# Thresholded attention, then a gated mixture of attentions: first-stage scores as three rounded products, exponential without a bias operand, fewer buffers, another order

## Chip, cores and metric

One core of a Trainium2 chip runs the whole kernel. The metric is the device time of one execution in microseconds, as the median of several runs. Engines: TensorE (PE in the profile, PEld its weight loads), VectorE (DVE), ScalarE (ACT), GpSimd (POOL) and SyncE (SP, which issues most DMAs).

## What is computed

`q`, `k`, `v` are 8 batches x 8 heads x 576 queries x 64. The first stage is an attention that keeps only scores within `tau` of the row's maximum. Its output, heads side by side, is the input `x` (576 x 512 per batch) of a second stage: a gate chooses 2 of 4 "experts" for each row, and every expert is a causal attention of its own with 64 columns.

```python
def _attn_ref(q, k, v, tau):
    scale = 1.0 / np.sqrt(q.shape[-1])
    scores = scale * np.matmul(q, k.transpose(0, 1, 3, 2))
    thresh = np.max(scores, axis=-1, keepdims=True) - tau
    scores = np.where(scores >= thresh, scores, -1000000000.0)
    scores = scores - np.max(scores, axis=-1, keepdims=True)
    attn = np.exp(scores)
    attn = attn / (np.sum(attn, axis=-1, keepdims=True) + 1e-09)
    return np.matmul(attn, v).astype(np.float32)
...
    for e in range(E):                     # second stage, E = 4
        q = x @ wq[e]
        k = x @ wk[e]
        v = x @ wv[e]
        scores = scale * (q @ k.transpose(0, 2, 1))
        scores = np.where(causal, -1000000000.0, scores)
        ...
        ye = a @ v @ wo[e]
        out += mask * w * ye               # w: softmax of the two chosen gate logits
```

## The kernel before

**Tiling.** Two heads of a batch are a pair, 32 pairs in all (`pair(n)`). Of a pair's 576 queries, 512 make four strips of 128 (`s` = 0 to 3). The last 64 queries of two successive pairs share a fifth strip (`s == R`), which is done with the odd pair, so there are 128 whole strips and 16 such shared ones, called tails below. A strip has two score rows of 576 keys, one for each head.

**One strip.** `prep` loads keys and queries, transposes them on PE (64 x 64 pieces against `ident`) and copies them out of PSUM with ACT into `kx` and `qx`; the copy of `qx` multiplies by `qsc`. `scores` multiplies them in plain float32: for each half of the keys (288 columns) and each head one matmul, with the two heads on the two halves of the array's rows. A float32 matmul stands in the trace as two instructions, so a strip shows 8. Then DVE copies the scores out of PSUM and takes their minimum (`copied_min`, tile `sc`; scores are negated), POOL adds `tau` (`thr`), ACT applies a kinked line (`kinked`, Prelu, which throws everything under the threshold far down) and the exponential with its row sum (`exp`, with the column `tau_n` = -tau as bias), DVE inverts the sum and POOL scales the row. `transp` transposes the probabilities on PE, DVE copies them out (tile `pt`), and `attnv` multiplies by `v`. Its result is split by ACT and DVE into a rounded high part and the low rest (tiles `x`), float32r both.

**The tail** multiplies 64 columns of weights by 288: four 64 x 64 corners of the array work at once, two heads by two pairs.

**Second stage.** `moe(b)` follows each four pairs. All its products are three float32r matmuls, high x high, high x low, low x high (`HHL`), added up in PSUM.

**Order.** Nothing runs in the order of the text. `Plan` records every operation with its tiles, `arrange` places them with a list scheduler, and the tables `PLACE` and `PLACE_OP` shift the due times of units ("os10" is strip 1 of odd pairs, "ACT kx" ACT's writes to `kx`). `SLOTS` says how many buffers a tile name has. Engines then execute their own queues in that order; a waiting instruction holds up all behind it. `fill` puts idle matmuls (`still`) into the first 80 us where the plan leaves PE empty.

The time falls into a start of some 82 us, in which only the first stage has work, and then batches of some 103 us, in which pairs of the next batch run between the products of the second stage.

Of the kernel before, what the change touches and what calls it, by code (L numbers as in the profile page):

```python
# [1213 lines left out]
```

## Time and profile before

| what | value |
|---|---|
| time, median of 3 runs | 859.16 us (858.79 to 859.38) |
| span of the profiled execution | 856.8 us |
| busy: PE, PEld, DVE, ACT, POOL | 827.5, 705.9, 621.1, 712.3, 350.6 us |
| mean granted TensorE clock | 0.994 of full speed |

The profiled execution has no time of its own beside its span; the median lies 2.4 us over that span. Busy time of PE counts the modelled tail of each matmul, so short gaps between matmuls do not show as idle: the start of the next instruction is the better measure of what one costs.

### The profile page before, as it was taken

To read this page: it belongs to the slowest core of one execution; us is meant where nothing else is said; L and a number is where in the kernel's file an instruction comes from. 1 tells how busy PE (TensorE), PEld (TensorE's weight loads), DVE (VectorE), ACT (ScalarE), POOL (GpSimd) and SP (SyncE) were. 2 spreads that over 40 slices of the span, in tenths; PEclk is the share of its full clock that TensorE was granted. 3 is DMA by queue.
4 is the path that set the end of the run, shared out by engine and by line. 5 is a ranking of instruction groups with operands and counts; after the bars stand their busy time and mean duration, and the time that the engine had idled before them with its cause. 6 is when DMAs were issued, how large, how long until landed. Compare 5 with 4: busy or idle time off the path is not lost.

```text
span 856.8 us, 28908 instructions
## 1 busy us (share of the span) xinstructions
PE 827.5 (97%) x11478; PEld 705.9 (82%) x11478; DVE 621.1 (72%) x1990; ACT 712.3 (83%) x1880; POOL 350.6 (41%) x607
## 2 busy tenths in 40 slices
PE   7999999999999999999999999999999999999998
PEld 5677888779887888878887788878888788887897
DVE  2787677776868677786777768687677776877565
ACT  5998889988789868897799977998878987789565
POOL 3665345443435334353244523344334443344211
PEclk8999999999999999999999999999999999999999
DMA  4442201130210302112021211312112031100002
GB/s 96 121 98 57 52 19 46 28 81 21 68 45 25 91 14 82 45 32 72 13 71 44 58 45 30 81 31 72 31 55 58 16 78 36 38 16 16 15 26 75
DMA packets 108103, 42.77 MB, mean 50 GB/s; under 512 B 94784, under 2 KB 103232, under 8 KB 107968
## 3 DMA queue, kind: packets, MB, share of 16 engines
q1 hardware_dynamic: 106624, 40.63, 18.5%
q8 instruction: 90, 1.47, 0.7%
q10 hardware_dynamic: 1344, 0.30, 0.2%
q14 instruction: 45, 0.37, 0.1%
HBM read 31.47 MB, written 9.44 MB: 48 GB/s over the span
## 4 chain that ended last, share of the span: by engine, by line
PE 69%; ACT 18%; DVE 6%; POOL 3%; issue 3%; SPq 0%; DMA 0%; POOLq 0%; DVEq 0%; ACTq 0%
PE banks L587 58%; PE banks L1183 10%; ACT pp L699 7%; ACT pp L693 7%; DVE sc L682 2%; DVE pt L623 2%; POOL pp L649 2%; PE banks L1180 1%; POOL p L649 1%; ACT p L693 1%; ACT pt L621 1%; ACT x L621 1%; DVE col L648 1%; ACT ptt L621 1%; POOL col L649 1%
## 5 line engine op out<-in xcount | busy, mean ns | idle before, releaser
L649 POOL TENSOR_SCALAR pp<-pp,col 128x576 f32<-128x576 f32 x288 | 212.6, 748 | 201.5 <-DVE col L660 119.4
L699 ACT ACTIVATE pp<-sc,col 128x576 f32<-128x576 f32 x288 | 211.1, 776 | 24.5 <-POOL col L649 23.2
L682 DVE TENSOR_SCALAR_CACHE_REDUCE sc<-banks 128x576 f32<-128x576 f32 x288 | 208.0, 751 | 21.0 <-PE banks L587 18.8
L693 ACT ACTIVATE pp<-pp,tau_n 128x576 f32<-128x576 f32 x288 | 222.5, 778 | 0.2
L623 DVE COPY pt<-banks 128x512 f32<-128x512 f32 x288 | 182.8, 682 | 8.8 <-PE banks L1183 8.3
L587 PE MATMUL banks<-kx,qx 64*128 64x288 f32 (+1 forms) x1280 | 179.1, 424 | 7.0 <-DVE pt L623 4.6
L587 PE MATMUL banks<-pt,vm 128*64 128x128 f32 (+1 forms) x2560 | 156.3, 266 | 0.1
L587 PEld LDWEIGHTS banks<-pt,vm 128*64 128x64 f32 x2560 | 131.1, 137 | 16.2 <-DVE sc L682 4.9
L587 PEld LDWEIGHTS banks<-kx,qx 64*128 64x128 f32 (+1 forms) x1280 | 101.8, 177 | 45.0 <-DVE pt L623 11.0
L649 POOL TENSOR_SCALAR col<-col,tau_p 128x2 f32<-128x2 f32 x144 | 38.9, 270 | 232.1 <-DVE sc L682 154.1
L1183 PE MATMUL banks<-ident,pp 64*128 64x64 f32 x2624 | 121.6, 227 | 7.7 <-DVE sc L682 3.3
L1183 PEld LDWEIGHTS banks<-ident,pp 64*128 64x128 f32 x2624 | 105.2, 139 | 28.3 <-POOL pp L649 5.6
L693 ACT ACTIVATE p<-p,col 128x512 f32<-128x512 f32 (+2 forms) x138 | 82.1, 604 | 18.3 <-DVE col L677 18.2
L649 POOL TENSOR_SCALAR p<-p,col,gw 128x512 f32<-128x512 f32 (+3 forms) x117 | 71.2, 619 | 44.3 <-DVE gw L632 30.2
L648 DVE TENSOR_SCALAR col<-col 128x2 f32<-128x2 f32 (+1 forms) x224 | 46.7, 212 | 57.3 <-ACT pp L693 49.8
L677 DVE CUSTOM_DVE_ANT_0 p<-banks,mask 128x512 f32<-128x512 f32 (+2 forms) x138 | 68.2, 514 | 21.4 <-PE banks L587 17.1
L632 DVE TENSOR_TENSOR x<-banks,x 128x256 fp32r<-128x256 f32 (+1 forms) x96 | 31.1, 351 | 58.1 <-ACT x L621 57.9
L621 ACT ACTIVATE pt<-banks 128x384 f32<-128x384 f32 (+2 forms) x128 | 57.5, 512 | 7.6 <-PE banks L1183 6.3
L587 PE MATMUL banks<-wvh,x 128*128 128x260 f32 x320 | 61.1, 285 | 0.0
L587 PE MATMUL banks<-ptt,vtz 128*64 128x128 f32 (+1 forms) x640 | 58.9, 263 | 0.0
L693 ACT ACTIVATION_READ_ACCUMULATOR pp<-pp,tau_n 128x1 f32 x288 | 58.3, 202 | 0.0
L587 PE MATMUL banks<-x,wkh 128*128 128x288 f32 x256 | 54.7, 307 | 0.0
(111 smaller groups left out, 1358.4 us busy)
## 6 DMA issues: line engine op xcount, KB each, us to landing
ki<-in_k_dram SPq DMA_DIRECT2D x64, 128.0 KB, 2.8
vm<-in_v_dram SPq DMA_DIRECT2D x32, 256.0 KB, 3.0
qi<-in_q_dram SPq DMA_DIRECT2D x62, 128.0 KB, 2.8
out_dram<-st SPq DMA_DIRECT2D x29, 256.0 KB, 2.5
tk<-in_k_dram SPq DMA_DIRECT2D x64, 32.0 KB, 2.2
vtz<-in_v_dram SPq DMA_DIRECT2D x64, 16.0 KB, 2.1
out_dram<-st SPq DMA_DIRECT2D x8, 128.0 KB, 2.3
tq<-in_q_dram SPq DMA_DIRECT2D x31, 32.0 KB, 2.3
```

The costliest lines, as they stand in the source:

```text
L587: lambda o, x, y: nc.tensor.matmul(o, x, y, start=start, stop=stop))
L621: run(e, t, [dst], [src], lambda d, s: nc.scalar.activation(d, s, AF.Copy))
L623: run(e, t, [dst], [src], lambda d, s: nc.vector.tensor_copy(d, s))
L632: lambda d, a, b: (nc.vector if e == "DVE" else nc.gpsimd).tensor_tensor(d, a, b, op=op))
L648: return m.tensor_scalar(d, s, x_, None, op0=op0)
L649: return m.tensor_scalar(d, s, x_, y_, op0=op0, op1=op1)
L677: lambda o, a, i, m: nc.vector.tensor_tensor_reduce(o, i, m, 1.0, 3e38, ALU.add, ALU.min, a))
L682: lambda o, a, i: nc.vector.tensor_scalar(o, i, 1.0, None, op0=ALU.mult, op1=ALU.min, accum_out=a))
L693: return nc.scalar.activation(d, s, AF.Exp, scale=scale, **kw)
L699: lambda d, s, x: nc.scalar.activation(d, s, AF.Prelu, bias=x, scale=-1.0, alpha=1e36))
L1180: nc.tensor.matmul(banks[:, n, :256], still_[:, :P], still_[:, :1].to_broadcast([P, 256]), start=True, stop=True)
L1183: o.fn(*(r.place() for r in (*o.outs, *o.ins)))
```

## The change

- `kx` and `qx` become float32r with two planes, high and low. ACT writes the high plane as before (now rounded), and DVE subtracts it from PSUM for the low plane: `minus` for the keys, `stt` (times `qsc`, minus high) for the queries. These are five new DVE instructions a pair.
- `scores` makes three float32r matmuls (`HHL`) in place of one float32 matmul, so a strip is 12 instructions, the two heads still side by side.
- The tail's queries go to constant tiles `qz0` and `qz1` of 128 columns, of which one half holds a pair's 64 last queries and the other stays zero. The tail becomes 24 matmuls with 128 columns of weights, six sums of two pairs into each bank. ACT writes them with one more copy a pair (64 columns); the first copy of `qx` falls from 320 columns to 256.
- `exp` has no bias in the first stage any more (`tau_n` is gone; the factor cancels in the division), and `tau_p` is cut at 80 instead of 104.
- `pt` has 4 buffers instead of 6, `x` 11 instead of 12.
- All numbers of `PLACE` and `PLACE_OP` are new.

```diff
+TOP = 80.0
-         ... "pt": 6, ... "x": 12, ...
+         ... "pt": 4, ... "x": 11, ...
 PLACE = {
-    "LMo0": 5.6250437, "LMo1": 7.2007713, ...
+    "LMo0": 13.27813, "LMo1": 8.710187, ...
...
     def exp(dst, src, bias=None, accum=None, scale=1.0):
+        ref = isinstance(bias, Ref)
...
-            if bias is not None:
+            if ref:
                 kw["bias"] = r.pop(0)
...
-    scaled("DVE", tau_p, tau_t, 0.0, 104.0, op0=ALU.max, op1=ALU.min)
-    scaled("DVE", tau_n, tau_p, -1.0)
+    scaled("DVE", tau_p, tau_t, 0.0, TOP, op0=ALU.max, op1=ALU.min)
...
+    qz = [const(f"qz{i}", [P, 2, P], F32R) for i in range(2)]
+    for t in qz:
+        memset("POOL", t.bitcast(F32), 0.0)
...
-        kx, qx = plan.tile("kx", [P, SM + 3 * ST], F32), plan.tile("qx", [P, SM + P], F32)
+        kx, qx = plan.tile("kx", [P, 2, SM + 3 * ST], F32R), plan.tile("qx", [P, 2, SM], F32R)
...
+                outs.append(([qz[n % 2][:, i, heads[n % 2]] for i in range(2)], gs[0][:, R * D:(R + 1) * D]))
+            for (hi, lo), src in outs:
+                copy("ACT", hi, src, None if x is ki else qsc)
+                if x is ki:
+                    minus("DVE", lo, src, hi.bitcast(F32))
+                else:
+                    stt(lo, src, qsc, hi.bitcast(F32), ALU.mult, ALU.subtract)
...
+        mm = [(q_[:, x], kx[:, y]) for q_, kx in qks for x, y in HHL]
         for hf in range(2):
-            for j, rows in enumerate(heads):
-                o = hf * HS + (ST if j == 0 else 0)
-                for i, (qx, kx) in enumerate(qks):
-                    if s < R:
-                        matmul(sp[j][:, hf, :HS], qx[rows, s * P:(s + 1) * P], kx[rows, o:o + HS], True, True)
-                    else:
-                        matmul(sp[j][heads[i], hf, :HS], qx[rows, SM:SM + ST], kx[rows, o:o + HS], True, True)
+            for i, (x, y) in enumerate(mm):
+                for j, rows in enumerate(heads):
+                    o = hf * HS + (ST if j == 0 else 0)
+                    matmul(sp[j][:, hf, :HS], x[rows], y[rows, o:o + HS], i == 0, i == len(mm) - 1)
...
-            exp(e, e, bias=tau_n, accum=ss[:, j:j + 1])
+            exp(e, e, accum=ss[:, j:j + 1])
```

PE around a tail in the middle of the run, before (`pp`, `p` are probabilities of the first and second stage being transposed; the last two rows come three times more):

```order
L587 MATMUL banks<-kx_67,qx_65 128x288 x4
L1183 MATMUL banks<-ident,p_80 128x64 x10
L1183 MATMUL banks<-ident,pp_70 128x64 x16
L1183 MATMUL banks<-ident,pp_69 128x64 x2
L1183 MATMUL banks<-ident,pp_70 128x64 x2
L1183 MATMUL banks<-ident,pp_69 128x64 x16
L587 MATMUL banks<-kx_68,qx_66 128x288 x4
L587 MATMUL banks<-kx_67,qx_65 64x288
L587 MATMUL banks<-kx_68,qx_66 64x288
```

and the same place in the change (the last two rows come once more):

```order
L588 MATMUL banks<-kx_67,qx_65 128x288 x12
L1190 MATMUL banks<-ident,p_78 128x64 x16
L1190 MATMUL banks<-ident,pp_70 128x64 x16
L1190 MATMUL banks<-ident,pp_69 128x64 x2
L1190 MATMUL banks<-ident,pp_70 128x64 x2
L1190 MATMUL banks<-ident,pp_69 128x64 x16
L1190 MATMUL banks<-ident,p_79 128x64 x10
L588 MATMUL banks<-q_108,q_107 128x128 x6
L588 MATMUL banks<-kx_68,qx_66 128x288 x12
L588 MATMUL banks<-kx_67,qz_182 128x288 x6
L588 MATMUL banks<-kx_68,qz_183 128x288 x6
```

A strip is 12 rows instead of 4 (each of the 4 is two instructions in the trace), the tail 24 instead of 8; around them the sequence is the same, but for one product of the second stage (`q_108,q_107`) that now stands between.

ACT where the next even pair is prepared, before (`sc` are scores, `col` threshold and row sum):

```order
L621 ACTIVATE kx_67<-banks 128x5x64 x2
L693 ACTIVATE p_80,col_135<-p_80,col_134 128x128
L699 ACTIVATE pp_71<-sc_81,col_147 128x576
L699 ACTIVATE pp_71<-sc_83,col_147 128x576
L693 ACTIVATE pp_71,col_141<-pp_71,tau_n 128x576 x2
L621 ACTIVATE pt_121<-banks 128x6x64 x2
L619 ACTIVATE qx_65<-banks,qsc 128x5x64
L619 ACTIVATE qx_65<-banks,qsc 128x4x64
```

and in the change:

```order
L622 ACTIVATE kx_67<-banks 128x5x64 x2
L695 ACTIVATE pp_69,col_142<-pp_69 128x576
L701 ACTIVATE pp_71<-sc_81,col_144 128x576
L701 ACTIVATE pp_71<-sc_82,col_144 128x576
L695 ACTIVATE pp_71,col_145<-pp_71 128x576 x2
L620 ACTIVATE qx_65<-banks,qsc 128x4x64 x2
L622 ACTIVATE pt_116<-banks 128x6x64 x2
L622 ACTIVATE pt_117<-banks 128x6x64 x2
L622 ACTIVATE ptt_93<-banks 128x3x64 x2
L620 ACTIVATE qz_182<-banks,qsc 128x64
```

The exponentials have lost their second input, and the copy into `qz_182` has come in.

DVE at the same place, before (a run of score copies, row-sum inversions and copies of transposed probabilities, `st` is an output tile):

```order
L682 TENSOR_SCALAR sc_83,col_142<-banks 128x576
L660 RECIPROCAL col_124<-col_124 128x2
L623 COPY pt_86<-banks 128x8x64 x2
L648 TENSOR_SCALAR col_135<-col_135 128x2
L660 RECIPROCAL col_135<-col_135 128x2
L682 TENSOR_SCALAR sc_84,col_148<-banks 128x576
L623 COPY pt_89<-banks 128x8x64 x2
L682 TENSOR_SCALAR sc_82,col_148<-banks 128x576
```

and in the change:

```order
L683 TENSOR_SCALAR sc_82,col_140<-banks 128x576
L633 TENSOR_TENSOR kx_67<-banks,kx_67 128x5x64 x2
L624 COPY pt_86<-banks 128x8x64 x2
L649 TENSOR_SCALAR col_142<-col_142 128x2
L683 TENSOR_SCALAR sc_83,col_132<-banks 128x576
L661 RECIPROCAL col_142<-col_142 128x2
L683 TENSOR_SCALAR sc_84,col_132<-banks 128x576
L649 TENSOR_SCALAR col_145<-col_145 128x2
L624 COPY st_75<-banks 128x512
L672 SCALAR_TENSOR_TENSOR qx_65<-banks,qsc,qx_65 128x4x64 x2
```

The two low planes of `kx` and the two of `qx` now stand between the score copies and the `pt` copies for which PE waits; the fifth (`qz_182`) follows some rows later.

## Rows read from the trace of the kernel before

**Rows 1.** Head of the page: span, busy time of each engine.
```profile
span 856.8 us, 28908 instructions
...
PE 827.5 (97%) x11478; PEld 705.9 (82%) x11478; DVE 621.1 (72%) x1990; ACT 712.3 (83%) x1880; POOL 350.6 (41%) x607
```

**Rows 2.** Windows: stretch, length, busy PE, PEld, DVE, ACT, POOL (instructions), clock, DMA.
```profile
0.00:82.00 82.00, 72.24 (x936) 55.65 (x936) 52.53 (x150) 68.11 (x161) 44.08 (x89) 0.94 0.41 95
489.00:560.50 71.50, 71.50 (x954) 62.37 (x952) 50.97 (x166) 56.67 (x156) 24.50 (x41) 1.00 0.21 56
560.50:589.40 28.90, 26.70 (x429) 21.81 (x429) 23.19 (x76) 28.00 (x70) 16.20 (x29) 1.00 0.10 27
582.10:593.20 11.10, 10.20 (x169) 8.11 (x166) 8.80 (x25) 11.02 (x30) 8.21 (x14) 1.00 0.29 70
```

**Rows 3.** Chain that ended last: one same piece, two batches apart (start, length).
```profile
386.73 4.67 PE banks L587 x88
...
592.99 4.67 PE banks L587 x88
```

**Rows 4.** Timeline of PE: start, length with overlap, operation, count [idle before].
```profile
399.70 0.43 PE L587 MATMUL banks<-x,wqh 128*128 128x288 f32 x2
399.96 0.30 PE L587 MATMUL banks<-x,wql 128*128 128x288 f32 x1
...
565.87 0.80 PE L587 MATMUL banks<-q,q 64*128 64x384 f32 x6
566.51 1.13 PE L587 MATMUL banks<-kx,qx 64*128 64x288 f32 x8
567.48 0.47 PE L1183 MATMUL banks<-ident,p 64*128 64x64 f32 x10
...
571.86 1.20 PE L587 MATMUL banks<-kx,qx 64*64 64x288 f32 x16 [0.63 <-DVE pt L623]
573.00 1.09 PE L587 MATMUL banks<-pt,vm 128*64 128x128 f32 x16
```

**Rows 5.** Windows, PE's score matmuls (tile kx) alone: busy and count.
```profile
489.00:560.50 71.50, 13.24 (x96) 1.00 0.21 56
560.50:589.40 28.90, 8.53 (x64) 1.00 0.10 27
```

**Rows 6.** Weight loads by shape: busy us, mean ns | idle before.
```profile
L1183 PEld LDWEIGHTS banks<-ident,pp 64*128 64x128 f32 x2624 | 105.2, 139 | 28.3 <-POOL pp L649 5.6 <-DVE sc L682 5.6 <-issue 3.2
L587 PEld LDWEIGHTS banks<-kx,qx 64*128 64x128 f32 x1024 | 93.4, 188 | 32.5 <-issue 9.0 <-ACT kx L621 2.2 <-DVE pt L623 2.0
```

**Rows 7.** ACT by shape: busy us, mean ns | idle before.
```profile
L693 ACT ACTIVATE pp<-pp,tau_n 128x576 f32<-128x576 f32 x288 | 222.5, 778 | 0.2
...
L621 ACT ACTIVATE x<-banks 128x256 fp32r<-128x256 f32 x64 | 24.3, 380 | 3.2 <-PE banks L587 3.0
...
L619 ACT ACTIVATE qx<-banks,qsc 128x256 f32<-128x256 f32 x32 | 16.0, 499 | 0.0
...
L693 ACT ACTIVATE p<-p,col 128x128 f32<-128x128 f32 x30 | 12.3, 410 | 0.1
...
L621 ACT ACTIVATE x<-banks 128x64 fp32r<-128x64 f32 x32 | 5.4, 224 | 11.3 <-PE banks L587 11.3
...
L693 ACT ACTIVATE gw<-lg 128x20 f32<-128x20 f32 x8 | 1.7, 217 | 4.9 <-DVE col L648 4.9
```

**Rows 8.** ACT's first-stage exponentials from 0 to 82 us, then from 560.5 to 589.4.
```profile
L693 ACT ACTIVATE pp<-pp,tau_n x35: 758/767/803, 13.0 to 81.3; 128x576 f32<-128x576 f32 x35
...
L693 ACT ACTIVATE pp<-pp,tau_n x14: 758/784/823, 564.7 to 588.7; 128x576 f32<-128x576 f32 x14
```

**Rows 9.** DVE by shape: subtractions that read PSUM, for the low part of x.
```profile
L632 DVE TENSOR_TENSOR x<-banks,x 128x256 fp32r<-128x256 f32 x64 | 26.7, 418 | 37.9 <-ACT x L621 37.8
...
L632 DVE TENSOR_TENSOR x<-banks,x 128x64 fp32r<-128x64 f32 x32 | 5.7, 218 | 20.2 <-ACT x L621 20.1
```

**Rows 10.** Waits of DVE, longest first: total us, times, longest.
```profile
DVE x L632 <- ACT x L621: 57.9, 40, 2.4
```

More of the change, by code (lines that the diff above doesn't have):

```diff
@@ L64 @@
-    "DVE gate": -1.7485447, "DVE gt": 0.628805, "DVE gw": 10.3278729, "DVE lg": 0.5485581, "DVE p2": 6.6361273,
-    "DVE pt": 0.6093573, "DVE q2": 6.1587626, "DVE qsc": 2.2242907, "DVE sc": 0.4147541, "DVE st": 2.0764245,
-    "DVE still": -5.1421316, "DVE tau_n": 2.1362434, "DVE tau_p": -1.7486267, "DVE v2": 9.3576526,
-    "DVE warm": 5.864085, "DVE x": -1.6190831, "DVE z0": 5.7182611, "DVE z1": -1.4953726, "DVE zt": 0.0879689,
-    "PE g": -2.26431, "PE s": -5.1211929, "POOL col": -2.9491708, "POOL ident": 11.3765455, "POOL mask": 2.1068493,
@@ L69 @@
-    "POOL mask2": -6.2814331, "POOL p2": 1.8110073, "POOL pp": 1.8121693, "POOL q2d0": 0.8758151,
-    "POOL q2d1": -0.1446924, "POOL st": -2.7509732, "POOL tie": -5.6142687, "POOL vtz0": -3.6496787,
-    "POOL vtz1": -1.8861265, "POOL wkl": 7.3932585, "POOL wol": 2.2351231, "POOL wql": 3.1951886,
-    "POOL wvh": 5.991101, "POOL wvl": -4.6781972, "SP ki": 0.7806451, "SP lg": -2.8207436, "SP out": -2.6560654,
-    "SP qi": 3.6633326, "SP st": 0.8889727, "SP tk": -4.2612691, "SP tq": -2.0309405, "SP vm": -3.0011593,
@@ L74 @@
-    "SP vtz0": -4.0909203, "SP vtz1": -5.6250596,
+    "ACT gw": 76.12253, "ACT kx": -71.61656, "ACT lg": 12.64471, "ACT p2": 70.27944, "ACT pp": 12.88868,
+    "ACT pt2": -24.60601, "ACT ptt": -30.48844, "ACT q2": -56.98534, "ACT q2d0": -42.78705, "ACT q2d1": 70.68693,
+    "ACT qi": -29.9186, "ACT qx": 58.09757, "ACT qz0": -3.248199, "ACT qz1": -34.02246, "ACT tau_t": -60.25753,
+    "ACT tq": 11.40594, "ACT v2": 42.4794, "ACT warm": 28.83537, "ACT wkh": 99.43994, "ACT woh": 32.68652,
+    "ACT wqh": 82.37161, "ACT wvh": -61.90852, "ACT x": -19.95029, "ACT z0": 63.44982, "ACT z1": 84.67473,
@@ new lines @@
+    "ACT zt": -1.653598, "DVE col": -5.890206, "DVE gate": -56.77737, "DVE gt": 2.615758, "DVE gw": 31.9327,
+    "DVE kx": 9.18084, "DVE lg": 18.31343, "DVE p2": 22.25444, "DVE pt": -4.528893, "DVE q2": 13.39019,
+    "DVE qsc": -89.92652, "DVE qx": 0.8551691, "DVE qz0": 35.07502, "DVE qz1": -30.29077, "DVE sc": 5.259721,
+    "DVE st": 57.56096, "DVE still": -67.26931, "DVE tau_n": -33.12211, "DVE tau_p": 4.176238, "DVE v2": -29.05777,
+    "DVE warm": 60.59643, "DVE x": 8.45129, "DVE z0": 70.14857, "DVE z1": 36.28226, "DVE zt": 37.01388,
@@ new lines @@
+    "PE g": -2.26431, "PE s": -5.121193, "POOL col": -25.49093, "POOL ident": -34.12438, "POOL mask": -19.65246,
+    "POOL mask2": 62.27128, "POOL p2": 1.914416, "POOL pp": 7.808766, "POOL q2d0": -92.67385, "POOL q2d1": 44.93355,
+    "POOL qz0": -52.83519, "POOL qz1": -31.25001, "POOL st": -19.31802, "POOL tie": 40.39643, "POOL vtz0": -0.9682185,
+    "POOL vtz1": 68.42984, "POOL wkl": 14.77641, "POOL wol": 31.02848, "POOL wql": -11.36127, "POOL wvh": -50.24941,
+    "POOL wvl": 26.03231, "SP ki": 0.7806085, "SP lg": 0.1613172, "SP out": -91.71912, "SP qi": 0.1122069,
@@ L75 @@
+    "SP st": 4.361411, "SP tk": -16.97103, "SP tq": 0.1488161, "SP vm": -6.555551, "SP vtz0": -4.472563,
+    "SP vtz1": -4.346254,
 }
@@ L690, in fn @@
             s = r.pop(0)
-            if bias is not None:
+            if ref:
                 kw["bias"] = r.pop(0)
             return nc.scalar.activation(d, s, AF.Exp, scale=scale, **kw)
-        run("ACT", cost("ACT", n, inps(src), accum is not None) + 100, [dst] + ([accum] if accum is not None else []),
-            [src] + ([bias] if bias is not None else []), fn)
+        run("ACT", cost("ACT", n, inps(src), accum is not None) + 100 * ref, [dst] + ([accum] if accum is not None else []),
+            [src] + ([bias] if ref else []), fn)
     def kinked(dst, src, x):
@@ L837, in prep @@
                 transposed(*gs, list(zip([*cs, tail], [tail, *cs])))
-                outs = ((o[:, ST:], 0, R + 1), (o[:, :SM + P], 0, R + 1))
+                outs = [([o[:, i, f:f + SM + P].rearrange("p (r c) -> p r c", c=P)[:, :, :D] for i in range(2)],
+                         g[:, :(R + 1) * D].rearrange("p (r c) -> p r c", c=D)) for f, g in zip((ST, 0), gs)]
             else:
                 transposed(*gs, [*((c, c) for c in cs), (tail, None)])
-                outs = ((o, 0, R + 1), (o, D, R))
-            for (d, at, m), g in zip(outs, gs):
-                d = d.rearrange("p (r c) -> p r c", c=P)[:, :m, at:at + D]
-                copy("ACT", d, g[:, :m * D].rearrange("p (r c) -> p r c", c=D), None if x is ki else qsc)
+                outs = [([o[:, i].rearrange("p (r c) -> p r c", c=P)[:, :, f:f + D] for i in range(2)],
+                         g[:, :R * D].rearrange("p (r c) -> p r c", c=D)) for f, g in zip((0, D), gs)]
+                outs.append(([qz[n % 2][:, i, heads[n % 2]] for i in range(2)], gs[0][:, R * D:(R + 1) * D]))
[5 more added lines that the diff above has]
+                    stt(lo, src, qsc, hi.bitcast(F32), ALU.mult, ALU.subtract)
         return (qx, kx, *values_in(n))
@@ L927, in pair @@
         qx, kx, vm, vt = prep(n)
-        held[n % 2] = (qx, kx), vm, vt
+        held[n % 2] = kx, vm, vt
         odd = n % 2
@@ L932, in pair @@
         for s in order:
-            pp[s] = scores(n, s, [held[i][0] for i in range(2)] if s == R else [(qx, kx)])
+            pp[s] = scores(n, s, [(qz[i], held[i][0]) for i in range(2)] if s == R else [(qx[:, :, s * P:(s + 1) * P], kx)])
         for s in order:
```

14 lines of the change are left out of this document (4 added, 10 removed), and 59 rows, old and new, of the table PLACE.

## Prediction, made before the changed kernel ran

> **What bounds the kernel now.** I read the head of the page first: PE is busy for 827.5 of 856.8 us, ACT for 712.3, DVE for 621.1 [rows 1]. An average over stages with different limits says little, so the windows came next. In the start, 0 to 82 us, ACT is busy for 68.1 us, which is all of the time from the first copies on, and PE has holes: ACT is the bound there [rows 2]. The chain shows the same piece at 386.73 and 592.99, two batches apart, so a batch takes (592.99 - 386.73) / 2 = 103.1 us [rows 3], and the 774.8 us behind the start are 7.5 batches. A batch has two parts. From 489.0 to 560.5 PE is never idle (71.50 of 71.50) and ACT is at 79%: PE is the bound. From 560.5 to 589.4 ACT is busy for 28.00 of 28.90, PE for 26.70: ACT is the bound, with PE only 2.2 us behind it [rows 2]. I call them the PE part and the ACT part. What the change is worth is read from each apart.
>
> **Score matmuls.** A whole strip in float32 begins at 566.51 and the next work at 567.48: 0.97 us [rows 4]. After the change it is six pairs of float32r matmuls with 288 columns. No row has that exact form. From below: projections with 288 columns on the full array start 0.13 us apart (two from 399.70 to 399.96), so a strip would be 0.78. From above: three pairs of the second stage with 384 columns and two heads take 0.64 us with their entry (565.87 to 566.51), 0.213 a pair, 0.16 if scaled to 288, so 0.96 [rows 4]. The three pairs hold a start-up that six share, so I take 0.80, near the lower end: 0.17 less per strip, 128 strips, -21.8 us of PE. The tail took 1.14 us (571.86 to 573.00) [rows 4] and becomes twelve pairs, 1.56 to 1.92; I take 1.64, 0.5 more, 16 times, +8.0. PE's whole balance is -13.8 us (ends -16 and +11). In the PE part stand 96 score instructions, which are 10 strips and a tail of 16; in the ACT part 64, which are 6 strips and a tail [rows 5]. So the PE part gets 10 x 0.17 - 0.5 = 1.2 us shorter. In the ACT part PE gets 0.5 us shorter, which is not the end there and counts nothing.
>
> **Exponential.** With bias it takes 778 ns for 576 columns and 410 for 128, 0.82 ns a column, so 321 for 20 columns; the gate's exponential, which has no bias, takes 217 for 20 [rows 7]. The bias costs 0.104 us. The bounds are 0 (if the row sum keeps that time) and 0.12 (what the column operand adds to a copy: 499 against 380 for 256 columns [rows 7]). The copy into `qz` adds 0.224 + 0.119 = 0.343 us a pair [rows 7]; the first `qx` copy loses a few hundredths, which I leave out. The ACT part holds 14 exponentials [rows 8] and one such copy: 14 x 0.104 - 0.343 = 1.1 us shorter. In the PE part ACT's relief hides behind PE and counts nothing.
>
> **Low planes on DVE.** Subtractions that read PSUM take 418 ns for 256 columns and 218 for 64, 1.04 ns a column [rows 9]: 0.485 for each of the two of `kx`, 0.418 for each of the two of `qx`, 0.218 for `qz`, 2.03 us a pair, 65 us in all. (The `qx` form with a column operand has no row that reads PSUM; with ACT's price for the operand it would be 0.54.) DVE goes from 621 to 686 us, about 81%. In the PE part PE's work covers this. At the end of the ACT part it is different: from 582.1 to 593.2 DVE is busy for 8.80 of 11.10 us [rows 2], and just there the order puts one pair's low planes between score copies and `pt` copies for which PE waits. Free are 2.3 us, needed 2.03. If all of it fits, it costs nothing; if none does, 2.0 us a batch. I take 0.5, nearer to the lower end because the order also moves rows out of that place.
>
> **Buffers, order, fillers.** Two `pt` buffers less bind PE's transposes more closely to `attnv`; in the PE part there is no idle that shows a shortage, and the bound is the ACT part's 2.2 us of PE idle once more [rows 2]. I take 0, covered by ACT, and keep 0 to 2.2 a batch for the range. Around the tails PE's sequence is the same as before, so the new tables cost 0. The idle matmuls of the start fall from 88 to 42; if that costs clock there (0.94 [rows 2]), ACT covers it.
>
> **Start.** 35 exponentials [rows 8] x 0.104 = 3.6 us less; copies into `qz` of about five pairs x 0.343 = 1.7 more; the first score now waits for the low planes of the first pair, about half of 2.03, 1.0 more. Together -0.9.
>
> **Sum.** A batch: -1.2 (PE part) - 1.1 (ACT part) + 0.5 (DVE) = -1.8, times 7.5 = -13.5; start -0.9; -14.4 us against the span of 856.8, 842.4. The median of the runs lies 2.4 over the span, so 859.2 - 14.4 = 844.8; I say 845.
>
> **Rivals.** (1) *DVE takes over the end of the ACT part.* A low plane waits for ACT's high plane, and the waiting instruction holds up the score copies and `pt` copies queued behind it, for which PE waits. The 96 subtractions for `x` show the price: 57.9 us of waits [rows 10], 0.60 each, so five a pair are 3.0 us, while only 0.3 of the free 2.3 remain after the work itself. Then the 2.0 us stand on the path and ACT's 1.1 gains nothing: -1.2 + 2.0 = +0.8 a batch, +6.0, with the start +5.1: 864. It decides as soon as more than 1.2 of the 2.0 us stay on the path. Against it: DVE idles for 1.76 us right ahead of that place, and waits are also filler of time that DVE had free. (2) *More goes.* If ACT's relief lets the order close PE's holes, the ACT part falls to PE's own work, 26.70 - 0.5 = 26.2, 2.7 less; with 1.2, 3.9 a batch, -29, with the start -30: 829. For it: ACT and PE are only 1.3 us apart there. Against: it needs POOL and DVE in time. (3) *Half of it goes*: DVE takes 1.6 instead of 0.5 a batch, -0.7, -5.3 and the start: 853. (4) *The exponential keeps an operand* (a constant column for the bias), so the change does not do what it says: the ACT part gets 0.3 longer, a batch -1.2 + 0.3 + 0.5 = -0.4, -3.0, start +2.7: 859, no change. (5) *Weight loads bound PE.* A strip has 12 loads instead of 8, a tail 24 instead of 16. At the mean of the present loads of that shape, 93.4 / 1024 = 0.091 us [rows 6], a strip would take 1.09 and a tail 2.19: 128 x 0.12 + 16 x 1.05 = +32: 891. Against it stand 2,624 loads of the same 128 columns for the transposes in 105.2 us, 0.040 each [rows 6]; at that price 12 loads are 0.48, hidden behind 0.80.
>
> The Trainium skill (TensorE: Matmul & The Clock Gate, section on LDWEIGHTS, loading the stationary operand) speaks against this change: it states that a load takes as many ns as it has columns, divided by 1.2, so 107 for 128. Were the loads to take turns at that, a strip would be 1.28 us and a tail 2.56, and my estimate from this page would be +62 us, 921. The trace disagrees with loads that take turns at that length: 0.040 us each for the transposes.
>
> **How the numbers follow.** Forecast, 838 to 851: 0.53. Rival 2: 0.17. Rival 3: 0.10. Rival 4: 0.05. Rival 1: 0.12. Rival 5: 0.03. Some 0.2% (1.7 us) is what a measurement of this kernel can tell from no change. Faster is the forecast with rivals 2 and 3, 0.80; same is rival 4, 0.05; slower are rivals 1 and 5, 0.15. The range leaves out the lower half of rival 2 and rivals 1 and 5: 831 to 860.
>
> **What would show it.** In the changed kernel's trace: strips that follow one another 0.80 us after their start and tails of 1.6 (wrong at 0.95 and more); exponentials of about 0.67 us and ACT busy for some 30 us less in them; DVE near 686 us; a batch of 101.3 us between same pieces of the chain, with an ACT part near 28. If DVE's waits on ACT's high planes stand in the chain, or PE's idle time in the ACT part names `pt` or the low planes of `kx` and `qx`, the sum is wrong there; if PE idles less than 1 us a batch, rival 2 holds.

## The result and the profile after

| kernel | median of its runs | ratio to the kernel before, 95% interval |
|---|---|---|
| before, beside it | 858.97 us (856.46 to 859.38) | |
| changed | 846.74 us (844.60 to 848.77) | 0.9869 [0.9844, 0.9894] |
| changed, second set (`again`) | 848.56 us | 0.9898 [0.9876, 0.9920] |
| changed, third set (`changed_again`) | 847.16 us (845.50 to 849.37) | 0.9877 [0.9858, 0.9896] |

The change makes the kernel 1.0 to 1.3% faster, by 8 to 12 us depending on the set; 845 was predicted, with 831 to 860 as the range. The kernel before took 855.5 to 857.7 us in 31 of its 44 executions beside the runs below, all with a mean granted clock of 0.995 or more, and 857.8 to 861.1 us in the others; three of the four executions in the first row lie in the longer range, and the trace of before, with a clock of 0.994, belongs there too. The page of the changed kernel begins as follows (head, busy time of each engine, granted clock in 40 slices, chain by engine and by line), and below it the chain of before:

```profile
span 847.1 us, 30291 instructions
...
PE 816.7 (96%) x12072; PEld 735.6 (87%) x12072; DVE 689.9 (81%) x2149; ACT 698.1 (82%) x1912; POOL 350.3 (41%) x609
...
PEclk8979999999999999999999999999999999999999
...
PE 60%; DVE 19%; ACT 12%; POOL 5%; issue 2%; DMA 0%; SPq 0%; POOLq 0%; DVEq 0%; ACTq 0%
PE banks L588 51%; PE banks L1190 9%; DVE sc L683 6%; DVE pt L624 4%; ACT pp L701 4%; ACT pp L695 4%; POOL pp L650 3%; ACT pt L622 2%; DVE col L649 2%; DVE st L624 2%; POOL p L650 1%; DVE qx L672 1%; ACT p L695 1%; DVE kx L633 1%; PE banks L1187 1%
```
```profile
PE 69%; ACT 18%; DVE 6%; POOL 3%; issue 3%; SPq 0%; DMA 0%; POOLq 0%; DVEq 0%; ACTq 0%
PE banks L587 58%; PE banks L1183 10%; ACT pp L699 7%; ACT pp L693 7%; DVE sc L682 2%; DVE pt L623 2%; POOL pp L649 2%; PE banks L1180 1%; POOL p L649 1%; ACT p L693 1%; ACT pt L621 1%; ACT x L621 1%; DVE col L648 1%; ACT ptt L621 1%; POOL col L649 1%
```

Against [rows 1] PE has lost 10.8 us and ACT 14.2, and DVE has gained 68.8; weight loads (PEld) rose to 87% and did not become the bound. In the chain DVE is now in second place with 19%, and it had 6% before. The clock line shows 0.8, 0.9, 0.7 and 0.9 in its first four slices of 21 us, and 0.9 or more (the highest digit) from there on. The mean clock is 0.986, and before it was 0.994.

The same piece of the chain, two batches apart (start, length, work):

```profile
505.49 9.23 PE banks L588 x88
...
707.69 9.23 PE banks L588 x88
```

That is (707.69 - 505.49) / 2 = 101.1 us a batch; before it was 103.1 [rows 3], and 101.3 was predicted. To compare kernels at the same place in the program I took the start of the n-th exponential of the first stage; there are 36 a batch. This table holds all the runs that the next section uses:

| kernel | 37th | 73rd | 253rd | last (288th) | us a batch, 73rd to 253rd |
|---|---|---|---|---|---|
| before | 90.40 | 188.62 | 703.37 | 798.86 | 102.95 |
| changed | 92.16 | 192.32 | 697.63 | 789.42 | 101.06 |
| `again` | 91.54 | 191.58 | 697.16 | 788.91 | 101.12 |
| `bias_back` | 93.20 | 194.61 | 704.81 | 797.93 | 102.04 |
| `no_low_planes` | 89.90 | 188.84 | 689.02 | 780.28 | 100.04 |
| `one_f32_product` | 89.12 | 190.73 | 708.06 | 801.71 | 103.47 |
| `before_no_bias` | 87.56 | 185.74 | 697.50 | 792.23 | 102.35 |
| `changed_again` | 90.50 | 190.66 | 696.28 | 788.00 | 101.12 |
| `still_at_gaps` | 88.95 | 188.26 | 693.87 | 785.64 | 101.12 |
| `still_at_gaps_again` | 88.40 | 187.66 | 693.57 | 785.38 | 101.18 |
| `before_few_still` | 90.72 | 188.97 | 703.78 | 799.27 | 102.96 |
| `old_tables` | 99.41 | 204.74 | 737.07 | 831.15 | 106.47 |
| `before_new_tables` | 88.53 | 188.08 | 709.49 | 804.59 | 104.28 |
| `before_fewer_buffers` | 88.83 | 187.06 | 701.85 | 797.35 | 102.96 |

The changed kernel is 1.8 us behind at the 37th exponential and 3.7 behind at the 73rd; in its other two traces (`again`, `changed_again`) it is 1.1 and 0.1 behind, then 3.0 and 2.0. So three traces of one kernel differ by 1.7 us in the start, and by 0.06 in the batch: a single trace shows a batch to 0.1 us, and the start not to better than 2. From the 73rd to the last one the changed kernel gains 13.1. So the batches bring what the forecast said or a little more, while the start loses where a small gain was forecast.

The windows over the same two batches, 145th to 217th exponential, first of before, then of the changed kernel (stretch, length, busy PE, PEld, DVE, ACT, POOL, clock, DMA):

```profile
394.75:601.00 206.25, 201.80 (x2854) 172.91 (x2849) 154.06 (x494) 176.31 (x467) 84.88 (x144) 1.00 0.19 49
```
```profile
394.46:596.23 201.77, 198.77 (x3010) 179.72 (x3008) 170.90 (x534) 172.58 (x476) 84.84 (x144) 1.00 0.19 50
```

PE's busy time fell by 3.0 and its idle time from 4.5 to 3.0, 4.5 us together in two batches (its other two traces are idle for 3.4 and 3.5 there). Within a batch the two parts of before [rows 2] are no longer so clear. Three stretches of the changed kernel show the start, one where DVE is nearest to full after PE, and one where ACT is:

```profile
0.00:82.00 82.00, 69.02 (x959) 58.50 (x961) 61.65 (x174) 66.34 (x166) 44.65 (x92) 0.90 0.41 96
...
523.30:544.60 21.30, 20.81 (x252) 18.21 (x252) 20.21 (x66) 18.84 (x54) 12.00 (x20) 1.00 0.30 82
566.80:587.60 20.80, 19.83 (x348) 17.24 (x350) 19.26 (x59) 20.31 (x56) 12.27 (x21) 1.00 0.18 46
```

**The operations.** PE's timeline, first of before (two strips, then the next work), then strip and tail of the changed kernel with what follows each (start, length with overlap, operation, count):

```profile
527.61 2.21 PE L587 MATMUL banks<-kx,qx 64*128 64x288 f32 x16
529.75 0.66 PE L587 MATMUL banks<-pt,vm 128*64 128x128 f32 x8
```
```profile
554.01 1.06 PE L588 MATMUL banks<-kx,qx 64*128 64x288 f32 x12
554.91 0.21 PE L1190 MATMUL banks<-ident,ki 64*128 64x64 f32 x1
...
566.84 1.86 PE L588 MATMUL banks<-kx,qz 64*128 64x288 f32 x24
568.54 0.69 PE L588 MATMUL banks<-q,q 64*128 64x384 f32 x6
```

A strip of before took (529.75 - 527.61) / 2 = 1.07 here, a strip of the changed kernel 554.91 - 554.01 = 0.90, a tail 568.54 - 566.84 = 1.70, and 1.14 before [rows 4]. Over all strips between 150 and 800 us the medians are 1.074 and 0.905. The changed kernel's exponential and the new low planes by shape (count, busy us, mean ns, idle before):

```profile
L695 ACT ACTIVATE pp<-pp 128x576 f32<-128x576 f32 x288 | 196.3, 688 | 0.3
```
```profile
L672 DVE SCALAR_TENSOR_TENSOR qx<-banks,qsc,qx 128x256 fp32r<-128x256 f32 x64 | 29.2, 476 | 8.0 <-ACT qx L620 7.9
...
L633 DVE TENSOR_TENSOR kx<-banks,kx 128x320 fp32r<-128x320 f32 x64 | 28.3, 480 | 0.0
...
L672 DVE SCALAR_TENSOR_TENSOR qz<-banks,qsc,qz 128x64 fp32r<-128x64 f32 x32 | 8.7, 272 | 0.0
```

The exponential went from 778 [rows 7] to 688 ns: the column operand cost 0.090 us. The low planes are 66.2 us of DVE, 65 was forecast.

### The profile page after: what moved, and what is told of

It reads as the page before. It is cut to its first block, busy times and chain, and to the rows that moved or that the text cites. A ratio compares the mean times of both kernels' runs of the same rounds, so it can differ in the third digit from the quotient of the medians.

```text
span 847.1 us, 30291 instructions
## 1 busy us (share of the span) xinstructions
PE 816.7 (96%) x12072; PEld 735.6 (87%) x12072; DVE 689.9 (81%) x2149; ACT 698.1 (82%) x1912; POOL 350.3 (41%) x609
## 4 chain that ended last, share of the span: by engine, by line
PE 60%; DVE 19%; ACT 12%; POOL 5%; issue 2%; DMA 0%; SPq 0%; POOLq 0%; DVEq 0%; ACTq 0%
PE banks L588 51%; PE banks L1190 9%; DVE sc L683 6%; DVE pt L624 4%; ACT pp L701 4%; ACT pp L695 4%; POOL pp L650 3%; ACT pt L622 2%; DVE col L649 2%; DVE st L624 2%; POOL p L650 1%; DVE qx L672 1%; ACT p L695 1%; DVE kx L633 1%; PE banks L1187 1%
## 5 line engine op out<-in xcount | busy, mean ns | idle before, releaser
L695 ACT ACTIVATE pp<-pp 128x576 f32<-128x576 f32 x288 | 196.3, 688 | 0.3
L588 PE MATMUL banks<-kx,qx 64*128 64x288 f32 x1536 | 146.1, 315 | 4.1 <-DVE sc L683 2.2
L588 PEld LDWEIGHTS banks<-kx,qx 64*128 64x128 f32 x1536 | 113.1, 189 | 25.4 <-DVE sc L683 8.4
L1190 PE MATMUL banks<-ident,pp 64*128 64x64 f32 x2640 | 117.0, 229 | 11.9 <-POOL pp L650 7.9
L1190 PEld LDWEIGHTS banks<-ident,pp 64*128 64x128 f32 x2640 | 101.1, 140 | 27.9 <-POOL pp L650 16.0
L650 POOL TENSOR_SCALAR p<-p,col,gw 128x256 f32<-128x256 f32 (+3 forms) x115 | 68.8, 607 | 60.5 <-DVE col L661 49.0
L695 ACT ACTIVATE p<-p,col 128x256 f32<-128x256 f32 (+4 forms) x136 | 80.6, 601 | 4.4 <-DVE col L678 3.5
L649 DVE TENSOR_SCALAR col<-col 128x2 f32<-128x2 f32 (+1 forms) x224 | 52.3, 240 | 25.8 <-ACT pp L695 20.4
L678 DVE CUSTOM_DVE_ANT_0 p<-banks,mask 128x256 f32<-128x256 f32 (+4 forms) x136 | 65.5, 511 | 7.3 <-PE banks L1190 7.1
L622 ACT ACTIVATE pt<-banks 128x384 f32<-128x384 f32 (+2 forms) x128 | 55.6, 509 | 17.8 <-PE banks L1190 17.8
L695 ACT ACTIVATION_READ_ACCUMULATOR pp<-pp 128x1 f32 x288 | 58.9, 204 | 0.0
L588 PE MATMUL banks<-x,wqh 128*128 128x288 f32 x256 | 53.8, 303 | 0.0
```

The costliest lines, as they stand in the source:

```text
L588: lambda o, x, y: nc.tensor.matmul(o, x, y, start=start, stop=stop))
L622: run(e, t, [dst], [src], lambda d, s: nc.scalar.activation(d, s, AF.Copy))
L649: return m.tensor_scalar(d, s, x_, None, op0=op0)
L650: return m.tensor_scalar(d, s, x_, y_, op0=op0, op1=op1)
L678: lambda o, a, i, m: nc.vector.tensor_tensor_reduce(o, i, m, 1.0, 3e38, ALU.add, ALU.min, a))
L695: return nc.scalar.activation(d, s, AF.Exp, scale=scale, **kw)
```

## Experiments

The theory is the forecast's sum: in a batch, faster strips and a lighter ACT gain in different parts, and low planes take a little back. The changed kernel ran beside the first three kernels as their measure:

> The changed kernel once more, on the chip and in the rounds of the three experiments beside it, so that they can be set against it: 0.987 of the kernel before, 846 to 848 us.

It took 848.56 us there, 0.9898 [0.9876, 0.9920] of before. The three each undo one part of it and leave the sequence on every engine as it is. That sequence was made for all parts together, so what a part is worth in them is its worth in this order.

**The bias back.** The exponential gets a column again (`tau_p`), the planner keeps the price without it.

```diff
-            exp(e, e, accum=ss[:, j:j + 1])
+            exp(e, e, bias=tau_p, accum=ss[:, j:j + 1])
```

> The changed kernel with a bias column on the first-stage exponentials again (the column of tau, whose factor cancels); the order of all engines is unchanged. ACT gets 288 x 0.10 = 30 us more work. My sum says that ACT's relief counts in the start (3.6 us) and in the ACT part (14 x 0.104 = 1.5 us in each of 7.5 batches): 11 to 15 us slower than the changed kernel. The rival that PE's products alone make the gain says 0 to 3 us slower.

Measured: 855.53 us, 7.0 more than the changed kernel on the same chip (848.56); ratio to before 0.9980 [0.9969, 0.9991]. That is less than the 11 to 15 expected and more than the rival's 0 to 3: ACT's relief counts, and neither all of it nor nothing. It is 1.7 us in the start, which is within the spread of single traces there, and (102.04 - 101.12) = 0.92 a batch, while 14 exponentials by 0.104 are 1.46. Its windows over the same two batches:

```profile
398.66:602.65 203.99, 199.16 (x3010) 179.72 (x3008) 171.54 (x534) 178.70 (x475) 84.80 (x144) 1.00 0.19 50
```

PE is idle for 4.8 us in them, and 3.0 to 3.5 without the operand. So most of the relief came out of PE's idle time.

**No low planes.** The subtractions write 4 columns a piece in place of 64, which leaves the low parts out of the products; the matmuls stay as many and as long, but read the high parts for all three products, and still wait for the short subtraction.

```diff
+                few = lambda a: a[:, :, :4] if len(a.shape) == 3 else a[:, :4]
...
-                    minus("DVE", lo, src, hi.bitcast(F32))
...
+                        lambda d, a, b, few=few: nc.vector.tensor_tensor(few(d), few(a), few(b), op=ALU.subtract))
...
-        mm = [(q_[:, x], kx[:, y]) for q_, kx in qks for x, y in HHL]
+        mm = [(q_[:, x], kx[:, y], q_[:, 0], kx[:, 0]) for q_, kx in qks for x, y in HHL]
```

> The changed kernel with the five subtractions of a pair done on 4 columns of each 64 only, and all three products taken from the high planes (so the low parts do not count in the result); the order is unchanged. DVE gets some 50 us less work. My sum charged DVE with 0.5 us a batch and 1 us in the start: 3 to 6 us faster than the changed kernel. The rival that DVE holds the end of the ACT part and ACT's relief with it says 10 to 20 us faster. If DVE is hidden, less than 1.

Measured: 839.73 us, 8.8 less than the changed kernel; ratio to before 0.9799 [0.9778, 0.9820]. That lies between the two expectations: low planes cost more than charged. What is left of them by shape, and the chain by engine:

```profile
L860 DVE SCALAR_TENSOR_TENSOR qx<-banks,qsc,qx 128x16 fp32r<-128x16 f32 x64 | 13.9, 226 | 8.6 <-ACT qx L624 7.2
...
L857 DVE TENSOR_TENSOR kx<-banks,kx 128x20 fp32r<-128x20 f32 x64 | 9.8, 171 | 2.0 <-ACT kx L626 0.5
...
L860 DVE SCALAR_TENSOR_TENSOR qz<-banks,qsc,qz 128x4 fp32r<-128x4 f32 x32 | 6.8, 211 | 0.8 <-ACT qz L624 0.6
```
```profile
PE 67%; ACT 17%; DVE 10%; POOL 3%; issue 2%; DMA 0%; SPq 0%; POOLq 0%; ACTq 0%; DVEq 0%
```

Of 66.2 us 30.5 are left, so 35.7 us less work on DVE gave 8.8 us. Both expectations counted on some 50, so the run does not show whether all of the low planes cost less than rival 1 said. In the trace it is 1.6 us in the start, again within its spread, and 101.12 - 100.04 = 1.08 a batch. The DVE share of the chain falls from 19 to 10%. What the part still there costs, the waits for ACT's high planes among it, this run does not tell.

**One float32 product for three.** The planes stand where they stood, but each three matmuls become one float32 matmul of the high parts, which again leaves the low parts out of the scores.

```diff
+        if whole is not None:
+            first, begin, end = whole
+            fn = (lambda o, x, y: nc.tensor.matmul(o, x.bitcast(F32), y.bitcast(F32), start=begin, stop=end)) if first else (lambda *_: None)
```

> The changed kernel with one float32 matmul of the high planes in place of each three float32r ones (the low parts do not count in the result); the order, the subtractions and the exponential are unchanged. A strip goes back from 0.80 to 0.97 us, a tail from 1.6 to 1.94: 128 x 0.17 + 16 x 0.34 = 27 us more on PE. My sum says that 10 of 16 strips and half of the tails count, in the PE part: 15 us slower than the changed kernel, up to 27 if PE is the bound everywhere. The rival that ACT's relief and the new order make the gain says less than 5.

Measured: 862.45 us, 13.9 more than the changed kernel, near the 15 expected and far from the rival's 5; ratio to before 1.0062 [1.0042, 1.0083]. The kernel with the lighter exponential and with the low planes, but without the faster strips, is slower than before. Its windows over the two batches, and its chain:

```profile
397.54:604.30 206.76, 205.22 (x2852) 176.82 (x2848) 170.28 (x534) 173.18 (x476) 84.73 (x144) 1.00 0.19 49
```
```profile
PE 81%; DVE 10%; ACT 4%; POOL 3%; issue 1%; DMA 0%; POOLq 0%; DVEq 0%; ACTq 0%
```

PE is idle for 1.5 us only. Strips have a median of 1.074 us again, and tails take 1.83, more than in either kernel; a batch is 103.47 - 101.12 = 2.35 longer. In the start this kernel is 2.4 us ahead, and its half-level stretches there are fewer (below).

**The exponential alone, in the kernel before.** Same edit the other way round, same sequence.

```diff
-            exp(e, e, bias=tau_n, accum=ss[:, j:j + 1])
+            exp(e, e, accum=ss[:, j:j + 1])
```

> The kernel before with its exponentials of the first stage without the pointer operand (which leaves the shift by tau out of the computation), all else and the order the same. Theory that ScalarE ends one part of each batch whatever TensorE does in the other: 14 exponentials by 0.10 us a batch, -1.0 to -1.4 us a batch, and 1 to 3 us in the start, -8 to -13 us in all. Rival: in the kernel before TensorE's f32 strips keep the exponentials waiting anyway and the relief counts only beside the faster strips: 0 to -3 us.

Measured: 852.20 us beside 857.40; ratio 0.9940 [0.9919, 0.9961]. It lies between theory and rival: 2.8 us in the start and 102.95 - 102.35 = 0.60 a batch. The trace of before has a stretch at the half clock level (33.6 to 37.0 us) that this one has not; against `before_fewer_buffers`, which runs the sequence of before and has no such stretch either, the start gains 88.83 - 87.56 = 1.3. In a kernel with slower strips less of ACT's relief reaches the end than in the changed one (0.92).

**The clock in the start.** The changed kernel shows the granted clock at its half level (1.2 GHz) in five stretches ahead of its end: 13.7 to 20.6 us, 41.0 to 47.9, 54.7 to 58.1, 82.0 to 85.4 and 126.4 to 129.8; before had two, 13.1 to 20.0 and 33.6 to 37.0. Windows of the changed kernel (`changed_again`), ahead of one fall, in it, and in the next, and what PE did ahead of it:

```profile
37.00:39.30 2.30, 0.61 (x13) 0.47 (x14) 2.30 (x8) 2.30 (x7) 1.74 (x3) 1.00 0.55 127
39.50:46.10 6.60, 6.56 (x91) 5.91 (x89) 5.87 (x13) 5.53 (x16) 4.26 (x7) 0.50 0.18 41
...
53.10:56.30 3.20, 3.20 (x29) 2.92 (x29) 2.82 (x8) 3.17 (x7) 1.63 (x3) 0.50 0.20 39
```
```profile
37.16 0.22 PE L1190 MATMUL banks<-ident,tq 64*128 64x64 f32 x1
39.07 0.68 PE L1190 MATMUL banks<-ident,pp 64*128 64x64 f32 x8 [1.69 <-POOL pp L650]
```

PE waited 1.69 us for POOL, then the clock halved, and PE was busy for 6.56 of the next 6.60 us: what had not been the bound became it. The sequence of before has 13 idle matmuls from 39.3 to 40.7 us alone and 57 behind its first 9 us; the changed kernel's last of 42 stands at 20.7. So the next kernel puts 52 more of them into PE's gaps of the changed kernel and moves nothing else (the two expectations below say 53; the numbers of the edit add up to 52, and the trace has 94 in place of 42).

```diff
+    pe = sorted(plan.when[n] for n in order if plan.ops[n].e == "PE")
+    for k, n in {314: 14, 436: 3, 463: 6, 554: 7, 734: 9, 772: 2, 1234: 7, 1244: 4}.items():
+        t = pe[k] - 0.5
...
+        idle += [(t + i * 1e-3, bank) for i in range(n)]
```

> The changed kernel with 53 more of the idle products on `still`, put where its trace shows TensorE idle ahead of a fall of the granted clock (39.0 to 40.7 us, 53.4 to 54.2, 62.7 to 63.6, 78.5 to 79.5, 81.3 to 81.7, 124.3 to 126.2); the order of the rest is the same. Theory that the start lost to the clock: the half level (1.2 GHz) that the changed kernel shows for 17 us of its first 130 us (41.0 to 47.9, 54.7 to 58.1, 82.0 to 85.4, 126.4 to 129.8), and the kernel before not, goes for the most part, the mean granted clock rises from 0.987 to 0.993 or more, and the time falls by 2 to 5 us against the changed kernel, since its start stood 1.7 us behind that of before at the 76th exponential. Rival, as the prediction had it: ScalarE covers it, the clock rises and the time stays within 1 us. Rival 3: idle time ahead is not what brings the clock down, the clock stays at 0.987 and the time too.

Measured: 844.97 us, ratio to before 0.9848 [0.9825, 0.9870], clock 0.996. Only 13.8 to 20.6 is left of the stretches. (The 76th exponential of this text and of the one below counts both operations of ACT on a row, the kinked line too; it is the 38th of the table's count. The 3.2 us of the text below are the trace of the changed kernel against this one there.) Then beside the changed kernel on the same chip:

> The changed kernel once more, as the measure for the others of this set: 846 to 849 us by its runs so far, mean granted clock 0.986 to 0.988.

> The changed kernel with the 53 idle products, beside the changed kernel on the same chip, to size what the clock in the start is worth: 2.5 to 4 us less than the changed kernel if the 3.2 us by which its 76th exponential stood earlier are kept to the end (no later stage gives them back); 1 us or less if a later stage does.

Measured: 847.16 us for the changed kernel and 844.91 (844.73 to 845.72) with the idle matmuls; ratios 0.9877 [0.9858, 0.9896] and 0.9853 [0.9834, 0.9873]. The intervals overlap and the gain of 2.3 us lies a little under the 2.5 that was expected, but at the 37th exponential it stands at 2.1 us, at the 73rd at 3.0 and at the last at 2.6, so it is kept. Of the 14 executions of the changed kernel in the three sets, two lie among the nine with the idle matmuls (844.4 to 845.7 us) and twelve above them. In the changed kernel alone the time goes with the clock in the same way: its two executions with a mean clock of 0.992 took 844.6 and 845.5, the four with 0.984 to 0.986 took 848.8 to 849.9. The same gap, filled, and the stretches from 40 to 60 us, without and with:

```profile
38.34 0.22 PE L1201 MATMUL banks<-ident,tq 64*128 64x64 f32 x1
39.01 1.71 PE L1198 MATMUL banks<-still 128*128 128x256 bf16 x14 [0.45 <-DVE qx L672]
```
```profile
40.00:50.00 10.00, 10.00 (x154) 9.29 (x152) 7.42 (x17) 8.05 (x23) 6.19 (x9) 0.69 0.35 76
50.00:60.00 10.00, 8.67 (x121) 7.67 (x119) 8.54 (x26) 7.55 (x20) 6.16 (x11) 0.83 0.50 126
```
```profile
40.00:50.00 10.00, 9.02 (x167) 7.63 (x164) 8.42 (x21) 8.47 (x23) 7.27 (x12) 1.00 0.27 62
50.00:60.00 10.00, 9.30 (x147) 7.73 (x149) 9.11 (x27) 8.68 (x23) 6.36 (x13) 1.00 0.63 147
```

ACT works for 17.2 us in these 20 with the clock kept, and 15.6 without. This is the fastest kernel of the study that computes the whole result.

**The counterpart in the kernel before**: the 57 later idle matmuls out.

```diff
-    idle = plan.fill(1250.0, 80000.0, 9000.0, 110.0, 217.0)
+    idle = plan.fill(1250.0, 9000.0, 9000.0, 110.0, 217.0)
```

> The kernel before with the 57 idle products taken out that it issues after its first 9 us (31 are left of 88). Theory that idle products hold the clock: the half level appears in the stretch from 20 to 90 us where before shows it for 3.4 us alone, mean clock falls from 0.994 to 0.985 to 0.990, and the time rises by 1 to 5 us. Rival: clock as before or lower, time within 1 us, since ScalarE ends the start.

Measured: 859.92 us (857.13 to 861.79), ratio 1.0020 [1.0006, 1.0035]. One stretch at the half level comes in (43.8 to 47.2 us) and the clock falls to 0.991, but in the profiled execution the last exponential is only 0.4 us late. The median says 2.5 us, the trace 0.4. The difference lies in the trace of before, which has a fall of its own at 33.6 us and a clock of 0.994: against `before_fewer_buffers`, the same sequence with one stretch only (14.4 to 17.8 us), the last exponential is 799.27 - 797.35 = 1.9 us late. The executions agree: eight of the ten without the 57 matmuls had a clock of 0.987 to 0.992 and took 858.7 to 861.8 us, two had 0.996 and took 857.1 and 857.4. So the price in the kernel before is some 2 us too.

**The tables.** The changed kernel with the order tables of the kernel before, and the other way round.

```diff
-    "LMo0": 13.27813, "LMo1": 8.710187, "LMo2": 21.0268, "LMo3": 3.909759, "LMo4": 4, "La00": 36.32976,
...
+    "LMo0": 5.6250437, "LMo1": 7.2007713, "LMo2": 5.4102597, "LMo3": 3.7853309, "LMo4": 4.0, "La00": 4.1671283,
...
```

> The changed kernel with the order tables of the kernel before (PLACE), so that only the new order is taken out; operations and buffers are those of the changed kernel, and the count of idle products follows the planner's gaps. Theory that the gain lies in the operations' prices and the order only follows them: +0 to +8 us against the changed kernel, still at or below the kernel before (848 to 856). Rival that the order carries the gain: +12 us or more, at or above the kernel before. Third: the tables are worth nothing, within 1.5 us.

> The kernel before with the order tables of the changed kernel, the counterpart of the changed kernel with the old tables, which took 45 us more than with its own. Theory that a table only fits the operations that it was tuned on: 10 to 45 us slower than the kernel before. Rival that the new table is better by itself, and the gain lies in it: at or below the kernel before (857), to 845.

Measured: 891.72 us, ratio 1.0382 [1.0349, 1.0415], and 864.51 us, ratio 1.0081 [1.0059, 1.0103]. Each table is worth having only with its own operations. The new operations under the old tables are 34 us slower than before, 45 over the changed kernel, so the rival's side (12 or more) and not the 0 to 8 that I expected; the old operations under the new tables lose 7.5, less than the 10 to 45 expected and clear of the rival. In the changed kernel with the old tables PE waits where it did not. Its matmuls of a strip by shape, the longest wait of the weight loads, and the two batches:

```profile
L588 PE MATMUL banks<-kx,qx 64*128 64x288 f32 x1536 | 142.8, 312 | 13.2 <-DVE pt L624 10.3 <-DVE sc L683 1.4 <-ACT ptt L622 1.2
```
```profile
PEld banks L588 <- DVE pt L624: 27.3, 37, 1.6
```
```profile
416.91:631.19 214.28, 204.09 (x3010) 183.42 (x3008) 167.53 (x535) 173.15 (x475) 84.99 (x144) 0.98 0.18 47
```

PE idles for 10.2 us in two batches instead of 3.0, with the copies into `pt` named first, and the granted clock, which was 1.00 in these batches of the changed kernel, falls there too (half level from 506.1 to 513.0 us). That this kernel has two `pt` buffers fewer than the tables were made for does not show as the reason: in its trace DVE's copies into `pt` wait for transposes (6.7 us in 16 waits) and never for the products that free a buffer. The old tables with six buffers were not run.

**The buffers.**

```diff
-SLOTS = {"ki": 2, "qi": 2, "qx": 2, "kx": 2, "pp": 5, "st": 2, "vm": 2, "p2": 3, "sc": 4, "pt": 6, "tk": 2, "tq": 2,
-         "ptt": 2, "x": 12, "v2": 1, "q2": 2, "zt": 2, "z0": 2, "z1": 2, "pt2": 4}
+SLOTS = {"ki": 2, "qi": 2, "qx": 2, "kx": 2, "pp": 5, "st": 2, "vm": 2, "p2": 3, "sc": 4, "pt": 4, "tk": 2, "tq": 2,
+         "ptt": 2, "x": 11, "v2": 1, "q2": 2, "zt": 2, "z0": 2, "z1": 2, "pt2": 4}
```

> The kernel before with 4 buffers for pt in place of 6 and 11 for x in place of 12, tables unchanged (the planner moves some rows by itself). By the prediction fewer buffers cost nothing, within 2 us; its own bound was 2.2 us a batch, +16 us, if transposes wait for pt; more than that would show the tables to hang on the number of buffers too.

Measured: 856.92 us, ratio 1.0003 [0.9988, 1.0018]. A batch takes 102.96 us and took 102.95: two buffers less for `pt` and one for `x` cost nothing in this order. The planner moved no row by itself: the sequence on DVE, ACT and POOL is that of before, and on PE but for matmuls that start together.

## Why the prediction was right, and where not

The forecast of 845 came out in time, with 846.7; of the gain of 14 us 8 to 12 came. Its mechanism held in kind for the batches and failed in the start; two terms of the batch were mis-sized and in part made up for each other.

That the time is so near is partly luck. The forecast counts from 859.2 us, and beside the later sets the kernel before took 856.7 to 857.4; from there the same sum gives 842 to 843, 4 to 6 us under what the changed kernel took there. On the spans of the two traces the change is 847.1 - 856.8 = -9.7 us where -14.4 was forecast, and the start makes the difference: at the 73rd exponential the trace is 3.7 us late where the sum has it 2.7 early, and behind it 13.4 are gained where the sum has 11.7.

- **Strips and tails: right.** 0.17 less a strip (1.074 to 0.905 in the median; my levels of 0.97 and 0.80 were both some 0.1 low, the difference was not; 0.97 was the shortest strip of before), tails 1.59 to 1.70 where 1.64 was said. (The lower end of PE's balance, -16, is -17.6 by the bounds given for strip and tail; nothing hangs on it.) PE's share of the gain is shown by `one_f32_product`. My split of it was too small: I counted PE's work in the PE part alone. By that the run would have lost 10 strips x 0.17 and one tail x 0.14, 1.8 a batch; it lost 2.35, of the 3.0 by which all its strips (2.7) and tails (0.3) are longer. In the changed kernel PE idles for only 1.5 to 1.7 us a batch, so most of what PE saves counts.
- **Exponential: right in kind, too large in size.** The operand costs 0.090, not 0.104 us. A batch gains 0.92 from it where 14 x 0.104 = 1.46 was put on the path, and the copies into `qz` taken off that. The Trainium skill (ScalarE: Activation LUTs, section What ACT_TABLE_LOAD costs) gives some 93 ns for each column operand of an ACTIVATE. The 90 ns measured here agree with it better than my 104 from the gate's exponential and 119 from the copies.
- **Low planes: work right, price too small.** 66.2 us on DVE for 65 said; but 0.5 a batch was charged, and 1.08 came back when a little over half of the work was taken away. The failing step is "nearer to the lower end because the order also moves rows out of that place": DVE ends 19% of the chain, and 6% before, in more places than the one that I looked at: score copies rose from 2 to 6% and copies into `pt` from 2 to 4, while the low planes of `qx` and `kx` are 1% each. Without most of the low planes (`no_low_planes`) these two are at 3% each. So rival 1 was right in that copies queued behind the low planes come late. Its price did not come: it counted 0.60 us of waiting for each low plane, and in the rows above DVE waits 7.9 us for ACT's plane of `qx` in the whole run and not for that of `kx`. The 1.08 lie inside the bounds of 0 to 2.0; what all of the low planes cost was not measured.
- **Sum of a batch: near, and not shown to add up.** -1.8 was forecast and 101.06 - 102.95 = -1.9 measured. The runs that undo one part each give -2.35 for the three products in strips and tails, -0.92 for the exponential and +1.08 for the part of the low planes that was taken out. In none of them are the longer tails (0.56 more than before, twice a batch, so up to 1.1), the copies into `qz`, the rest of the low planes and the order, and the three were each measured in the presence of the others. What does add up is PE's own account in the windows above: in a batch it is busy for 1.5 us less and idle for 0.5 to 0.7 less.
- **Start: wrong.** -0.9 was forecast, and the 37th exponential came 0.1 to 1.8 us late in three traces, the 73rd 2.0 to 3.7. The failing step is the sentence on the idle matmuls, "if that costs clock there ..., ACT covers it". It cost clock in four stretches, and ACT did not cover it: filled gaps gave 2.1 us back by the 37th exponential and 3.0 by the 73rd. With them the 37th is at 88.40, 2.0 ahead of the trace of before but only 0.4 ahead of `before_fewer_buffers`, so whether the rest of the start's sum holds stays open. Between the 37th and 73rd exponential the changed kernel takes 100.2 us and before 98.2. The fill accounts for 0.9 of this, and the low planes for about 1.1: `no_low_planes` takes 98.9 there where `again` takes 100.0.
- **Tables: wrong as a term.** "The new tables cost 0" can't be tried apart from the operations: these alone, under the old tables, are 34 us slower than before, and the new tables alone are 7.5 slower. The forecast's sum silently assumed an order that fits the new operations.
- **Buffers: right**, shown in the kernel before: 0.0 a batch.
- **Weight loads: right to reject.** Twelve loads and twelve matmuls of a strip fit in 0.905 us, 0.075 for a load with its matmul. By what the Trainium skill (TensorE: Matmul & The Clock Gate, section LDWEIGHTS) gives for a load of 128 columns, my estimate for loads that take turns was 1.28 us a strip. The trace disagrees with loads that take turns.

## What to carry to other kernels

Where one engine is close to full in all parts of the program, most of what it saves counts (here 2.35 of 3.0 us a batch), and a second engine's relief or load counts at some share; undo each part alone, at the same place in the sequence, to get that share. Read it from the batches: in the start, traces of one and the same kernel differed by 1.7 us here. An order tuned to one set of operation times is part of the kernel: an operation that is faster by itself can lose by far more than it gains in the order made for its slower form. After a change that leaves TensorE idle in new places, read the granted clock over the first stages, and try to fill the gaps that stand ahead of a fall.
